# Where a decode kernel's forward loop issues its pair sums, its projection matmuls and its small ScalarE copies

## Chip, cores and metric

The kernel runs on one core of one Trainium2 chip. The metric is the device time of one execution in microseconds; the time before is the median of five runs. A profile of one execution, taken by the hardware profiler, stands beside it.

## What is computed

One token is decoded through an adaptively normalised block, forward and backward. `mod = silu(c) @ w_mod` gives six vectors (shifts, scales, gates). Attention has 32 heads of width 192 over a cache of 8192 keys and values; a second block is a two-layer GELU network with gate. The outputs are the result and the gradients of nine inputs, those of the key and value caches (100 MB each) among them.

```python
h = layernorm(x) * (1 + ca) + sa
q = (h @ wq)                                  # 32 heads of 192
p = softmax(einsum(q, k_cache) * 192 ** -0.5)
x = x + ga * ((p @ v_cache) @ wo)
h = layernorm(x) * (1 + cb) + sb
x = x + gb * B(h)                             # B: x1 = x + ..., x1 + gelu(layernorm(x1) @ w3) @ w4
```

## The kernel before

**Two parts.** A forward part (about 0 to 545 us) streams K and V once, head by head; then come a short dense part (the network and its gradient, to about 590 us) and a backward part, which reads V again and writes both cache gradients. The change lies in the forward part and in the short stretch that ends it.

**Tiling.** A head's 8192 positions lie as 128 partitions by 64. K and V come in two halves of 1536 KB each (`load_k`, `load_v`, on the SP queue). K has a ring of five such buffers, V of three. The weights of a pair of heads (`wo`, 480 KB) and of four heads (`wq`, 960 KB), and chunks of `w_mod` (960 KB), come on the same queue; `wq` and `w_mod` share one buffer.

**Order.** The engines' queues hold exactly the written order (`manual_schedule`). Iteration i of the loop (L504 to L590) works on three heads at once: x = head i (scores), y = head i - 1 (softmax, V scaling, first three quarters of the products with V), z = head i - 2 (last quarter, output). In one iteration:

- VectorE multiplies a half of K by q (`dot_mul`, L297), adds the two halves of the width (`dot_half`, L302); TensorE sums with identity matmuls (`dot_tree`, L308); VectorE reduces the rest (`dot_sum`, L312). This is done for two halves, `pa` and `pb`.
- The maximum goes over the partitions by a matmul into the tile `mx` (L520), and VectorE takes the negative maximum (L526); ScalarE computes the exponentials (L343).
- `scale_v` (L346 to L370) multiplies a quarter of V by the exponentials, nine of 16 steps on VectorE (L356), seven on ScalarE (L363). Tiles `vs`, three buffers.
- `m_quarter` (L387) takes one scaled quarter: TensorE accumulates the 192 by 192 products of K and V in the PSUM tile `mp` (L378, L383) and the head's output in the PSUM tile `op` (L395), the "o bank", of which 193 of 256 columns are used. The tiles `mp` and `op` have two buffers each.
- `m_out` (L419) copies both to SBUF with ScalarE (L414, L416, L422); `m_add` (L425) adds a part on VectorE (L427).

**Once per pair of heads**, at odd i ("last"): `pair_sums` (L436) runs `pair_sum` for both heads, ten fp32 matmuls with one output column (L432 to L434), into a PSUM tile `po` of the one-buffer pool psS. `pair_o` (L442) on VectorE normalises (L444 to L448); `pair_ao` (L451) multiplies with `wo` on TensorE (L455, into `ao_ps`, pool psS), and ScalarE copies the result into `AO` (L557).

**Once per four heads**, at i = 3, 7, ...: `q_half` (L262) runs twice, five matmuls each into `q_ps` (L265; pool psB, one buffer, shared with `mx`), and a scaled ScalarE copy into `qs_bc` (L267), from which the heads i + 1 to i + 4 take their q. At i = 1, 5, 9, `mod_blocks` (L237) does the like for six columns of mod (L241, L242).

**Where these stand.** `pair_sums` and the first `q_half` stand ahead of `m_quarter(1)`. The L557 copy and the second `q_half` or `mod_blocks` stand between `scale_v(2)` and `scale_v(3)`. The loads in an iteration are: K of i + 1, first half (after `m_quarter(3)` of z); V of i, second half (after `scale_v(1)`); K of i + 1, second half (after `m_quarter(1)`); wo, wq or w_mod; V of i + 1, first half. Each waits for the last reader of its buffer, in that order, on SP's one queue.

```python
if last:
    po = pair_sums((os_.pop(i - 3), os_.pop(i - 2)))
if i % 4 == 3 and wch is not None:
    q_half((i + 1) // 4, 0, wch)
if y is not None:
    m_quarter(1, y["k"][0], vs1, y["mp"], y["op"])
nx["k"].append(load_k(i + 1, 1))
```

## Time and profile before

| | |
|---|---|
| median of five runs | 1447.58 us (1443.05 to 1459.39) |
| profiled execution, its own time | 1443.59 us |
| its span, first to last instruction | 1441.8 us |
| mean granted TensorE clock | 0.723 |
| busy in the span: TensorE, VectorE, ScalarE | 83%, 77%, 61% |
| DMA | 571.96 MB, mean 397 GB/s |
| L363, V scaling on ScalarE | 840 of 443 ns, 303.2 us |
| L297, K times q on VectorE | 62 of 3352 ns, 207.8 us |
| L378 and L383, K times V on TensorE | 1920 of 254 ns and 1920 of 251 ns (overlapping), 294.2 us |

The profile counts a matmul as busy to its modelled end, so neighbouring matmuls overlap and the time from start to start is shorter than the mean of one. A line of the timeline gives start, duration, engine, source line, operation, tiles and count, and in brackets the engine's idle time before it and what released it. A line of the waits gives who waited for whom, the total in microseconds, how often, and the longest. Granted clock is TensorE's, as a share of full speed.

### The profile page before, as it was taken

How to read it: one execution, taken by the hardware profiler on the slowest of the kernel's cores; microseconds unless marked ns; L12 is line 12 of the kernel's file. 1: busy time of each engine (PE TensorE's matmuls, PEld its weight loads, DVE VectorE, ACT ScalarE, POOL GpSimd, SP SyncE). 2: the span in 40 equal slices, each digit the busy share in tenths (PEclk: the TensorE clock that was granted, in tenths of full speed). 3: DMA queues.
4: the chain of work that ended last, by engine and by line, in shares of the span. 5: the costliest groups of instructions: out<-in, count | busy, mean ns of one | idle time of the engine just before them, and what ended most of it. 6: DMA issues, size and time to landing. Idle time of an engine off the chain costs nothing.

```text
span 1441.8 us, 29963 instructions
## 1 busy us (share of the span) xinstructions
PE 1194.5 (83%) x12577; PEld 783.8 (54%) x12577; DVE 1109.7 (77%) x1395; ACT 881.2 (61%) x1923; POOL 138.0 (10%) x240
## 2 busy tenths in 40 slices
PE   3999999999999988877888877789887888678874
PEld 1677777677777767544444444445444444344442
DVE  4999999999999997676667676766676677567684
ACT  0777767676777773554555665566566556455654
POOL 0000000000000000121111110111111111011111
PEclk9999999999999997575555555555556556555555
DMA  9999999999999996599999999999999999999998
GB/s 375 398 410 409 415 413 416 390 396 400 391 397 405 410 415 256 200 401 422 418 400 412 422 413 417 418 414 414 408 416 423 425 423 411 370 377 417 400 399 348
DMA packets 77748, 571.96 MB, mean 397 GB/s; under 512 B 8590, under 2 KB 26718, under 8 KB 37294
## 3 DMA queue, kind: packets, MB, share of 16 engines
q1 hardware_dynamic: 51402, 343.59, 59.2%
q0 software_dynamic: 26192, 226.47, 38.0%
q8 instruction: 98, 1.61, 0.4%
q14 instruction: 36, 0.29, 0.0%
q10 hardware_dynamic: 20, 0.00, 0.0%
HBM read 343.58 MB, written 225.91 MB: 395 GB/s over the span
## 4 chain that ended last, share of the span: by engine, by line
PE 44%; DVE 28%; ACT 13%; issue 7%; DMA 7%; POOL 1%; SPq 0%; ACTq 0%; POOLq 0%; DVEq 0%
PE dot_ps L938 18%; DVE prod L297 8%; PE dv_ps L949 6%; DVE pq L929 6%; ACT vs L363 5%; PE wT_ps L816 4%; PE mp L378 4%; DMA out_dram<-KB 3%; DVE prod L302 3%; DVE vs L356 3%; PE dot_ps L308 3%; ACT KB L950 2%; ACT wT L817 2%; PE mp L383 2%; DVE S_h L312 2%
## 5 line engine op out<-in xcount | busy, mean ns | idle before, releaser
L950 ACT CAST KB<-dv_ps 128x768 bf16<-128x768 f32 x504 | 382.4, 803 | 273.7 <-PE dv_ps L949 272.8
L938 PE MATMUL dot_ps<-pq,ident_bf 128*128 128x256 bf16 x1536 | 356.6, 401 | 65.9 <-DVE pq L929 65.6
L363 ACT ACTIVATE vs<-VB,Ef 128x192 bf16<-128x192 bf16 x840 | 303.2, 443 | 0.0
L938 PEld LDWEIGHTS <-ident_bf 128*128 128x128 bf16 x1536 | 188.3, 133 | 189.3 <-issue 128.9
L949 PE MATMUL dv_ps<-do_r,er_b 1*128 1x192 bf16 x2048 | 219.6, 334 | 59.0 <-ACT KB L950 53.2
L954 DVE TENSOR_TENSOR KB<-qs_bc,dS 128x3072 bf16<-128x3072 bf16 x126 | 220.6, 1752 | 24.9 <-DMA out_dram<-KB 19.0
L929 DVE TENSOR_TENSOR pq<-VB,do_r 128x3072 bf16<-128x3072 bf16 x126 | 220.6, 1750 | 0.0
L297 DVE TENSOR_TENSOR prod<-KB,qs_bc 128x6144 bf16<-128x6144 bf16 x62 | 207.8, 3352 | 9.5 <-DMA KB<-in_A_k_cache_dram 4.9
L378 PE MATMUL mp<-vs,KB 128*128 128x193 bf16 x1920 | 190.6, 254 | 0.0
L949 PEld LDWEIGHTS <-er_b 1*128 1x128 bf16 x2048 | 91.9, 111 | 176.8 <-issue 168.9
L378 PEld LDWEIGHTS <-KB 128*128 128x128 bf16 x1920 | 170.9, 101 | 17.4 <-issue 3.9
L312 DVE TENSOR_REDUCE dP<-dot_ps 128x32 f32<-128x512 f32 x64 | 44.2, 690 | 141.5 <-PE dot_ps L938 141.5
L793 POOL DMA_DIRECT2D er_b<-er_t x64 | 40.9, 639 | 1163.4 <-PE w3T_ps L666 576.9
L308 PE MATMUL dot_ps<-prod,ident_bf 128*128 128x512 bf16 x372 | 94.4, 392 | 44.6 <-DVE prod L302 44.6
L356 DVE TENSOR_TENSOR vs<-VB,E 128x1728 bf16<-128x1728 bf16 x120 | 123.6, 1051 | 0.0
L302 DVE TENSOR_TENSOR prod<-prod 128x3072 bf16<-128x3072 bf16 x62 | 108.6, 1752 | 0.6
L817 ACT COPY wT<-wT_ps 128x1024 bf16<-128x1024 bf16 x84 | 80.8, 961 | 45.1 <-PE wT_ps L816 42.1
L383 PE MATMUL mp<-vs,KB 128*64 128x193 bf16 x1920 | 103.6, 251 | 0.0
L383 PEld LDWEIGHTS <-KB 128*64 128x64 bf16 x1920 | 77.6, 110 | 20.1 <-issue 20.1
L308 PEld LDWEIGHTS <-ident_bf 128*128 128x128 bf16 x372 | 34.7, 99 | 86.2 <-issue 58.2
L1187 POOL DMA_DIRECT2D out_dram<-KB x127 | 68.3, 542 | 43.6 <-ACT KB L950 16.1
L343 ACT ACTIVATE E<-S_h,negm 128x256 bf16<-128x256 f32 x30 | 15.2, 508 | 85.7 <-DVE negm L526 85.7
(333 smaller groups left out, 1015.6 us busy)
## 6 DMA issues: line engine op xcount, KB each, us to landing
VB<-in_A_v_cache_dram SPq DMA_DIRECT2D x125, 1536.0 KB, 11.0
out_dram<-KB POOLq DMA_DIRECT2D x125, 1536.0 KB, 14.5
KB<-in_A_k_cache_dram SPq DMA_DIRECT2D x64, 1536.0 KB, 10.3
wo_st<-in_A_wo_dram SPq DMA_DIRECT2D x30, 480.0 KB, 8.6
w_st<-in_A_wq_dram SPq DMA_DIRECT2D x12, 960.0 KB, 13.2
out_dram<-wo_st POOLq DMA_DIRECT2D x16, 480.0 KB, 19.3
out_dram<-w_st POOLq DMA_DIRECT2D x7, 960.0 KB, 21.2
w_st<-in_w_mod_dram SPq DMA_DIRECT2D x6, 960.0 KB, 18.1
```

The lines of the kernel that those rows point to most:

```text
L297: V_.tensor_tensor(out=prod, in0=src, in1=vec[:, None, :].to_broadcast([P, JH, DH]), op=ALU.mult)
L302: V_.tensor_tensor(out=prod[:, :, 0:w], in0=prod[:, :, 0:w], in1=prod[:, :, w : 2 * w], op=ALU.add)
L308: T_.matmul(ps, lhsT=ident_bf, rhs=prod[:, :, k : k + TS], start=(k == 0), stop=(k == w - TS))
L356: V_.tensor_tensor(out=vs[:, 0:n, 0:DH].rearrange("p j (a b) -> p j a b", b=4), in0=v[:, v0 : v0 + n, :].rearrange("p j (a b) -> p j a b", ...
L363: A_.activation(out=vs[:, k, 0:DH], in_=v[:, v0 + k, :], func=ACT.Copy, scale=Ef[:, j0 + k : j0 + k + 1])
L378: T_.matmul(mp[:, 0:MW], lhsT=kb[:, j0 + k, 0:P], rhs=vs[:, k, 0:MW], start=(q == 0 and k == 0), stop=(z and k == JQ - 1), skip_group_chec ...
L383: T_.matmul(mp[p0 : p0 + 64, MO : MO + MW], lhsT=kb[:, j0 + k, P:DH], rhs=vs[:, k, 0:MW], start=False, stop=(z and k >= JQ - 2), skip_grou ...
L929: V_.tensor_tensor(out=pq[:, q], in0=v_l[s][:, q * JQ : (q + 1) * JQ, :], in1=do_of(ht(s)[0])[:, None, :].to_broadcast([P, JQ, DH]), op=AL ...
L938: T_.matmul(ps[:, q * JQ : (q + 1) * JQ, :], lhsT=ident_bf, rhs=pq[:, q, :, k : k + TS], start=(k == 0), stop=(k == DH - TS), skip_group_c ...
L949: T_.matmul(ps[:, b, k * DH : (k + 1) * DH], lhsT=er[p0 : p0 + 1, 2 * m + k, :], rhs=doh[p0 : p0 + 1, :], start=True, stop=True)
L950: A_.copy(out=dV4[:, 2 * q : 2 * q + 2, m * PW : (m + 1) * PW], in_=ps[:, :, 0:PW])
L954: V_.tensor_tensor(out=dK[:, lo:hi, :].rearrange("p j (a b) -> p j a b", b=4), in0=qh.rearrange("p (a b) -> p a b", b=4)[:, None, :, :].to ...
```

## The change

- `pair_sum` runs for one head in every iteration from i = 2 on: at even i for head i - 2, at odd i for the other head of the pair. It stands after `m_quarter(1)` and after the issue of the second K load. It writes columns 200 to 205 of the o bank of the pair's second head, without the start flag; `po` is a view of that bank, and the tile in psS is no longer used.
- At odd i, `pair_o` stands after `dot_half(pb)` and its tree instead of before them.
- The first q half is computed at i = 3, 7, ..., the second at the next (even) i, and mod blocks at i = 2, 6, 10, each with its matmuls between the second dot tree and `m_quarter(2)`.
- The copies into AO, `qs_bc` and `mod` are issued after `scale_v(3)`.
- In the stretch that ends the forward part, the sums of the last two pairs, the second part of head 30's `o_rows`, `pair_o` and `pair_ao` change places.

```diff
-    def mod_blocks(b0, nb, w):
+    def mod_mm(nb, w):
...
+        return ps
+
+    def mod_out(b0, nb, ps):
         A_.copy(out=mod[:, b0 : b0 + nb], in_=ps[:, 0:nb])
...
-    def q_half(n, b, w):
+    def q_mm(b, w):
...
+        return ps
+
+    def q_out(n, b, ps):
         lo = n * CW + b * PW
         A_.activation(out=qs_bc[:, lo : lo + PW], in_=ps[:, 0:PW], func=ACT.Copy, scale=SCALE)
...
-        def pair_sum(po, b, os_h):
+        def pair_sum(po, b, os_h, start=True):
             rows = slice(64 * b, 64 * b + 64)
             for k in range(3):
-                T_.matmul(po[rows, k : k + 1], lhsT=os_h[:, k:DH:3], rhs=c32[:, 0:1], start=True, stop=True)
...
+                T_.matmul(po[rows, k : k + 1], lhsT=os_h[:, k:DH:3], rhs=c32[:, 0:1], start=start, stop=start, skip_group_check=True)
...
-        def pair_sums(os2):
-            po = psS.tile([P, 8], FP32, name="po", tag="s")
-            for b in range(2):
-                pair_sum(po, b, os2[b])
-            return po
...
                 early(i, "mid")
-                if last:
-                    po = pair_sums((os_.pop(i - 3), os_.pop(i - 2)))
-                if i % 4 == 3 and wch is not None:
-                    q_half((i + 1) // 4, 0, wch)
                 if y is not None:
                     m_quarter(1, y["k"][0], vs1, y["mp"], y["op"])
                 nx["k"].append(load_k(i + 1, 1))
+                if z is not None:
+                    po = (z if last else y)["op"][:, 200:208]
+                    pair_sum(po, i % 2, os_.pop(i - 2), start=False)
+                late = []
                 pb = dot_mul(x["k"][1], qh)
                 if z is not None:
                     m_add(i - 2, z["mp"], mt)
+                dot_half(pb)
+                x["d1"] = dot_tree(pb, psR, DH // 2)
                 if last:
                     o2 = pair_o(t, po)
-                dot_half(pb)
-                x["d1"] = dot_tree(pb, psR, DH // 2)
                 if y is not None:
                     vs = scale_v(2, y["v"][1], E4, Ef)
                 if last:
-                    A_.copy(out=AO[:, :, 2 * t : 2 * t + 2], in_=pair_ao(o2, wo_l.pop(t)))
+                    ps_ao = pair_ao(o2, wo_l.pop(t))
+                    late.append(lambda ps=ps_ao, t=t: A_.copy(out=AO[:, :, 2 * t : 2 * t + 2], in_=ps))
                 if i % 4 == 3 and wch is not None:
-                    q_half((i + 1) // 4, 1, wch)
+                    late.append(lambda ps=q_mm(0, wch), n=(i + 1) // 4: q_out(n, 0, ps))
+                if i % 4 == 0 and wch is not None:
+                    late.append(lambda ps=q_mm(1, wch), n=i // 4: q_out(n, 1, ps))
                     wch = None
-                if i % 4 == 1 and wch is not None:
-                    mod_blocks(mb, nb, wch)
+                if i % 4 == 2 and wch is not None:
+                    late.append(lambda ps=mod_mm(nb, wch), lo=mb, n=nb: mod_out(lo, n, ps))
...
                     y["vs"] = scale_v(3, y["v"][1], E4, Ef)
+                for f in late:
+                    f()
                 nx["v"].append(load_v(i + 1, 0, VB[(2 * i + 2) % NVB]))
...
-                if i == H1 - 1:
-                    po = psS.tile([P, 8], FP32, name="po", tag="s")
-                    pair_sum(po, 0, os_.pop(H1 - 3))
...
             score_tree(1, d1)
+            pair_sum(po, 1, os_.pop(H1 - 2), start=False)
             dot_sum(d0, x["S"][:, 0:JH])
             m_add(H1 - 2, z["mp"], mt)
-            o_rows(H1 - 1, vy, op_y, JH, J)
-            o_out(H1 - 1, op_y, es, os_)
...
             mx = row_max(x["S"])
-            po_x = psr([P, 8], FP32, "po_x")
-            pair_sum(po_x, 0, os_.pop(H1 - 1))
+            o_rows(H1 - 1, vy, op_y, JH, J)
+            o2 = pair_o(TL - 1, po)
             negm = neg_max(mx)
             A_.activation(out=E_all[:, H1, :], in_=x["S"], func=ACT.Exp, bias=negm[:, 0:1], scale=1.0)
+            o_out(H1 - 1, op_y, es, os_)
+            ps_ao = pair_ao(o2, wo_l[TL - 1])
+            A_.copy(out=AO[:, :, 2 * TL - 2 : 2 * TL], in_=ps_ao)
+            po_x = psr([P, 8], FP32, "po_x")
             op_x = psO.tile([P, 256], FP32, name="op")
...
-            pair_sum(po, 1, os_.pop(H1 - 2))
-            o2 = pair_o(TL - 1, po)
+            pair_sum(po_x, 0, os_.pop(H1 - 1))
             pair_sum(po_x, 1, os_.pop(H1))
             er_t = [e_rows(TL, psB, "b")]
-            ps_ao = pair_ao(o2, wo_l[TL - 1])
             w3t(1)
             o2 = pair_o(TL, po_x)
-            A_.copy(out=AO[:, :, 2 * TL - 2 : 2 * TL], in_=ps_ao)
```

## The prediction

> **What bounds the kernel now.** I began with the page's slices of the span.

> ```profile
> ## 2 busy tenths in 40 slices
> PE   3999999999999988877888877789887888678874
> ...
> DVE  4999999999999997676667676766676677567684
> ...
> PEclk9999999999999997575555555555556556555555
> DMA  9999999999999996599999999999999999999998
> ```

> The change touches only the forward loop over heads, the first fifteen slices (0 to 545 us). There TensorE, VectorE and DMA all read nine tenths, so busy shares don't tell which of them is the bound. The waits between 65 and 543 us do:

> ```profile
> ACT AO L557 <- PE ao_ps L455: 39.1, 14, 4.6
> PE dot_ps L308 <- DVE prod L302: 29.7, 32, 1.8
> ACT qs_bc L267 <- PE q_ps L265: 21.1, 14, 3.0
> DVE rz L444 <- PE po L434: 13.7, 14, 1.2
> DVE S_h L312 <- PE dot_ps L308: 6.4, 7, 1.6
> ```

> VectorE waits 13.7 us for the pair sums (14 times) and 6.4 us for dot trees (7 times), and almost nowhere else. ScalarE's two large waits cost VectorE nothing directly. So VectorE sets the pace, broken by TensorE once per pair. Next, stretches of one pair each (an odd head and the even one after it; us, length, busy PE, PEld, DVE, ACT, POOL, then granted clock, DMA share, GB/s):

> ```profile
> 304.87:338.96 34.09, 31.74 (x455) 24.79 (x451) 32.27 (x32) 24.22 (x77) 0.00 (x0) 0.95 0.97 383
> 338.96:374.18 35.22, 33.15 (x463) 25.19 (x459) 32.36 (x32) 25.18 (x79) 0.00 (x0) 0.95 1.00 404
> 374.18:407.43 33.25, 29.93 (x451) 23.27 (x449) 32.11 (x31) 24.21 (x77) 0.00 (x0) 1.00 0.99 395
> 475.87:509.44 33.57, 31.51 (x461) 24.18 (x459) 32.34 (x32) 25.18 (x79) 0.00 (x0) 1.00 1.01 417
> ```

> VectorE's work is the same 32.1 to 32.4 us; the lengths differ by the clock. The fourteen pairs from i = 3 last 35.17, 34.63, 33.57, 34.62, 33.57, 34.54, 33.58, 34.09, 35.22, 33.25, 35.18, 33.26, 33.57 and 34.16 us. Clock 0.95 stands at i = 3, 5, 9, 13, 17, 19, 23. In slices of 0.2 us each of these is one stretch of half clock, 3.4 us long, begun during or just after the pair sums (316.2 to 319.8 at i = 17). Last, the timeline of TensorE and VectorE in a pair at full clock (i = 21):

> ```profile
> 382.96 0.52 PE L395 MATMUL op<-vs,ones_bf 128*32 128x193 bf16 x16
> 383.41 0.69 PE L432 MATMUL po<-c,osb 128*64 128x1 f32 x6
> ...
> 385.50 0.38 PE L434 MATMUL po<-osb,c 128*128 128x1 f32 x2
> 385.75 1.51 PE L378 MATMUL mp<-vs,KB 128*128 128x193 bf16 x16
> ...
> 388.42 1.47 PE L308 MATMUL dot_ps<-prod,ident_bf 128*128 128x512 bf16 x6
> ```

> ```profile
> 384.63 0.35 DVE L427 TENSOR_TENSOR M<-mp,mt 64x193 f32<-64x193 f32 x1
> 385.92 0.18 DVE L444 RECIPROCAL rz<-po 128x3 f32<-128x3 f32 x1 [0.94 <-PE po L434]
> ...
> 386.48 1.75 DVE L302 TENSOR_TENSOR prod<-prod 128x3072 bf16<-128x3072 bf16 x1
> 388.14 1.05 DVE L356 TENSOR_TENSOR vs<-VB,E 128x1728 bf16<-128x1728 bf16 x1
> ```

> Both heads' sums stand ahead of the second quarter (L378), and VectorE's in-order queue stands 0.94 us at the reciprocal with its half-add behind it.

> [...]

> **The change, part by part.**

> *Half clock.* [...] So I take the stretches as gone. Their price, against full-clock pairs with q matmuls (33.57) and without (33.25): 1.60 + 1.65 + 1.61 at i = 3, 19, 23; 1.38 + 1.37 + 0.84 at i = 5, 9, 17; 1.29 - 0.5 = 0.8 at i = 13, whose even head has the small operations of L475 to L480. Sum 9.25 us. Ends: 0 if they stay; 9.25.

> *The wait for po.* A walk through i = 21: the second quarter starts at 383.41, lasts 2.67 (385.75 to 388.42), so to 386.08. ScalarE's part of it was done at 383.84, before the tenth of 16 steps needs it. The sum takes 1.11: 387.19, seen by VectorE 0.04 later, 387.23. VectorE has the M add at 384.63, the half-add from 385.01 (0.38 on, as elsewhere), 1.66 more: 386.67. Wait 0.56 in place of 0.94: the wait moves, it doesn't go. 14 x 0.38 = 5.3 us. Ends: 0 (the quarter waits for all of ScalarE's scaling) and 14 x 0.94 = 13.2. Late next is nothing: the dot tree needs the half-add (386.67) and starts at 387.2, 1.2 earlier than now.

> *Even heads.* Their sum stands ahead of their second dot tree, which waits 0.65 us for VectorE at i = 22; the tree comes 0.4 us later, and the reduction that reads it has about a microsecond of room (tree done at 302.9, reduction at 304.0 at i = 16). Zero; without that cover 0.4 x 14 = 5.6.

> *q and mod matmuls.* The same number, one half in each of two heads. Full-clock pairs with q are 0.32 longer; TensorE idles 3.3 us in a pair without, so half of each hides. I take half of 7 x 0.25: 0.9 us. Ends 0 and 2.2.

> *ScalarE copies behind the V scaling.* The waits of 39.1 and 21.1 us shrink, off VectorE's path: nothing by itself. Behind the late q copy wait VectorE's product of head 4n (it reads qs_bc) and the mx matmul, which shares q_ps's bank; scaling ends about 320.5 in a head that ends at 322.5, so the copy at 320.7 to 321.2 has 1.3 us of room. If that is gone, 7 times the excess.

> *Queues.* On SP the second K load follows the second quarter, 2.3 us earlier (3.4 where the clock was halved: issued at 320.35, and 172 to 233 GB/s in the three microseconds after 320). The wo load follows ao, 1.2 earlier, the V load the scaling, 1.5 to 2 earlier. At i = 2, 6, 10 the wq load, and at i = 4, 8 the w_mod load, now wait on SP for a matmul group of their own head, with a V load behind that would wait for the scaling anyway: nothing. POOL issues nothing here.

> *Tail.* Head 30 loses its sum ahead of mx (544.54 to 545.5) and gets one ahead of a tree that waits 0.65; a VectorE wait of 0.58 at 549.64 goes. The later sums and pair_o swap places of equal length. Gain 0.4, ends -0.5 and 0.6.

> VectorE's sum: 9.25 + 5.3 + 0.9 + 0.4 = 15.9 us.

> *What DMA lets through.* The pairs from i = 3 to 9 (with w_mod loads) moved 56.7 MB in 138.0 us. At the densest pair's 417 GB/s that takes 136.0; at 425, which single slices show in the backward part, 133.4. VectorE would save 6.1 there; I allow 3.3, so 2.8 are lost. The later ten moved 137.2 MB in 340.4 us; at 417 that is 329.0, room for 11.4 where VectorE saves about 9.5. Total 15.9 - 2.8 = 13.1 us. Against the profiled execution: 1443.59 (span 1441.8 and 1.8 around it) to 1430.5. That execution is 4.0 below the median of the five; the median's counterpart is 1447.58 - 13.1 = **1434.5**.

> **Rivals.**
> *No DMA limit:* all 15.9 and up to 3 more of the po wait: 1430. For: K transfers never hold VectorE now. Against: 417 is the best of all pairs.
> *The po wait stays or some half clock stays:* half of 9.25 to all of it, nothing else: gain 5 to 9, 1440. [...] Against: the steps start before ScalarE has ended (PE at 311.43 with scaling to 311.96).
> *It doesn't do what it says:* DMA share is 1.00 throughout, so earlier loads only queue and VectorE meets late K: 1446. Against: dry microseconds such as 320 to 323.
> *Slower:* every one of 29 sums starts a half-clock stretch. At 9.25 / 7 = 1.3 us each, 29 x 1.3 = 38 less 15.9: 1470. It needs over 12 stretches to cancel the gain from the other terms, 23 for 1% slower. Against: thin stretches are half as long as now.

> **How the numbers follow.** Forecast 0.46 (own range 1430 to 1438), no DMA limit 0.17, part stays 0.20, nothing 0.08, slower 0.09. Below 1427 and above 1448 I leave about 0.17. One per cent, 14.5 us, is about what a measurement of this kernel can tell from no change. Below 1433.1 lie the no-limit case and half of the forecast: 0.40. Slower by over 1%: 0.08. The rest, 0.52, is within.

> **What would show it.** Right: granted clock 1.00 in all pairs, L444's wait about 0.56 each, no wait at L312, pairs near 32.9 after i = 11, no dry microseconds after the second K load, ScalarE's waits at AO and qs_bc gone. Wrong: half-clock stretches, or VectorE waiting for K transfers in more than the early pairs.

## The result, and the profile after

Each median is over the runs of its own series. The changed kernel takes 1436.65 us (38 runs, 1427.98 to 1448.33), the kernel before, measured beside it, 1446.75 us (75 runs). The ratio on record is 0.9937, with a 95% interval of 0.9923 to 0.995, so 0.6% faster; the quotient of the two medians is a little lower, 0.993. The medians differ by 10.1 us where 13.1 were forecast. The prediction of 1434.5 is 2.2 us low. The profiled execution of the changed kernel took 1433.29 us, with a span of 1431.5; it is 3.4 us below its median, as the one before was 3.2 us below its own.

The slices of the changed kernel's span, to be read against those of before: the first fifteen are the forward loop.

```profile
## 2 busy tenths in 40 slices
...
PEclk7999999999999997755555566565555557555565
...
GB/s 374 405 419 418 419 411 412 413 413 407 418 413 409 418 382 217 238 365 425 421 422 416 419 400 410 423 416 420 409 413 410 421 421 413 419 385 411 402 411 343
```

No forward slice is below 405 GB/s between the second and the fourteenth; before, several were between 390 and 400. A half-clock stretch of 3.4 us in a slice of 36 us is too short for the digit to show it, so the clock has to be read pair by pair. VectorE's waits between 65 and 535 us in the changed kernel (us in all, times, longest):

```profile
DVE rz L444 <- ACT vs L369: 5.1, 10, 0.6
DVE prod L303 <- DMA KB<-in_A_k_cache_dram: 4.9, 9, 1.5
DVE prod L303 <- PE dot_ps L314: 1.7, 1, 1.7
DVE negm L526 <- PE mx L520: 1.2, 1, 1.2
DVE rz L444 <- PE op L440: 0.9, 1, 0.9
```

The wait for the pair sums is 6.0 us instead of 13.7, and the 6.4 us for dot trees are gone. Nine waits for a K transfer are new, and so is the one at L303 for a dot tree; it belongs with the one at L526 (below), where before there were 0.6 us in two places. ScalarE's wait ahead of the AO copy fell from 39.1 us to 1.6, ahead of the q copy from 21.1 to 0.2. ScalarE isn't busier for it: its wait for the negative maximum, ahead of the exponentials, rose from 65.2 to 120.5 us (28 times each), off VectorE's path.

The label "ACT vs L369" in the first row is not the cause. The changed kernel's timeline of the pair i = 21, in order of start:

```profile
376.44 1.52 PE L384 MATMUL mp<-vs,KB 128*128 128x193 bf16 x16
...
377.78 2.53 ACT L369 ACTIVATE vs<-VB,Ef 128x192 bf16<-128x192 bf16 x7
...
378.03 1.76 DVE L308 TENSOR_TENSOR prod<-prod 128x3072 bf16<-128x3072 bf16 x1
...
379.86 0.38 PE L440 MATMUL op<-osb,c 128*128 128x1 f32 x2
...
380.35 0.18 DVE L444 RECIPROCAL rz<-op 128x3 f32<-128x3 f32 x1 [0.56 <-ACT vs L369]
```

ScalarE's scaling ends at 377.78 + 2.53 = 380.31, by coincidence beside the end of the sum; as the loop repeats, so does the coincidence. The test is the distance that does not change: L444 starts 0.49 us after the start of L440 here, and again at 346.87 to 347.36 and 412.85 to 413.34. In experiment e1_sums, where the sum is late and ScalarE was done 0.48 us earlier, it is 0.49 too (348.90 to 349.39), and there the profile names "PE op L440". So VectorE waits for the sum. The reader also sees the new order: quarter (L384), one sum (which ends with L440), and VectorE's half-add (L308) now ahead of the reciprocal instead of behind it.

Pairs of the changed kernel (start and end, length, busy PE, PEld, DVE, ACT, POOL, granted clock, DMA share, GB/s):

```profile
166.41:201.34 34.93, 30.82 (x481) 24.10 (x479) 32.39 (x32) 24.27 (x78) 0.00 (x0) 1.00 1.01 413
334.21:367.20 32.99, 30.54 (x452) 23.46 (x447) 32.21 (x31) 24.70 (x79) 0.00 (x0) 1.00 1.02 419
...
499.15:535.60 36.45, 32.51 (x458) 25.04 (x456) 32.51 (x32) 25.05 (x81) 0.00 (x0) 0.95 0.97 382
```

The thirteen from i = 3 last 34.17, 33.74, 33.42, 34.93, 33.41, 33.50, 32.98, 32.98, 32.99, 32.99, 32.99, 32.98 and 32.99 us, all at clock 1.00. From i = 15 on they are equal to a hundredth, with q matmuls (the row from 334.21) or without (from 367.20, 32.99 us with 461 matmul records, not shown). The first six are longer, though VectorE's and TensorE's work is nearly the same (32.39 and 30.82 us in the first row). Five of them, i = 3 to 11, hold all the K waits; the w_mod loads are issued at heads 0, 4 and 8. The sixth, i = 13, has no K wait but more work of VectorE's own (32.76 us), the small operations that the prediction names. The last row has the only half-clock stretch of the forward loop from head 3 on, and it is longer than its counterpart before.

The two profiled executions by stretch: up to head 3, 65.19 us before and 65.08 after; heads 3 to 29, 444.25 and 434.07 (-10.18); from head 29's first product to du_bf, the end of the work that depends on the forward loop, 70.18 and 73.02 (+2.84); the rest about -2.8. The rest is not touched by the change, and from the write of dao_bf to the end its length varies between 852 and 866 us over the profiles of this study, so -2.8 there is no finding.

What went wrong at the end of the loop shows in the changed kernel's timeline there:

```profile
500.94 0.28 PE L174 MATMUL bc_t<-ident_f,dbo 128*5 128x128 f32 x1
...
502.61 0.21 PE L181 MATMUL bc_ps<-bc_rows,ident_bf 5*128 5x128 bf16 x1 [0.67 <-ACT w4b L182]
...
503.17 0.49 PE L520 MATMUL mx<-ident_f,m 128*128 128x128 f32 x2 [0.35 <-ACT w4b L182]
...
503.50 2.63 PE L384 MATMUL mp<-vs,KB 128*128 128x193 bf16 x16
...
503.70 0.29 DVE L526 TENSOR_REDUCE negm<-mx 128x1 f32<-128x128 f32 x1 [1.20 <-PE mx L520]
...
509.28 3.36 DVE L303 TENSOR_TENSOR prod<-KB,qs_bc 128x6144 bf16<-128x6144 bf16 x1 [1.69 <-PE dot_ps L314]
```

At the end of head 28 the kernel broadcasts the columns of dbo (L174 to L182): TensorE and ScalarE hand over to each other four times, and in that time TensorE does little (0.28 us of the transpose, 0.38 us of a group of four that is not shown, and 0.21, in the 1.9 us from 500.94 to 502.82). Head 28 is a multiple of four, so its second half of q and its sum now stand on TensorE's queue ahead of this. The mx matmuls come late, VectorE waits 1.20 us for them; the quarter behind runs at half clock (2.63 us for what takes 1.5); the dot tree comes late by that, and the next product, which needs the tree's buffer, waits 1.69 us.

### The profile page after: what moved, and what is told of

Same layout as the page of the kernel before. It is cut to its first block, busy times and chain, and to the rows that moved or that the text cites. A ratio compares the mean times of both kernels' runs of the same rounds, so it can differ in the third digit from the quotient of the medians.

```text
span 1431.5 us, 29992 instructions
## 1 busy us (share of the span) xinstructions
PE 1186.7 (83%) x12577; PEld 776.7 (54%) x12577; DVE 1109.7 (78%) x1395; ACT 878.1 (61%) x1923; POOL 137.9 (10%) x240
## 3 DMA queue, kind: packets, MB, share of 16 engines
q8 instruction: 98, 1.61, 0.4%
## 4 chain that ended last, share of the span: by engine, by line
PE 38%; DVE 33%; DMA 11%; ACT 8%; issue 8%; POOL 1%; SPq 0%; ACTq 0%; POOLq 0%; DVEq 0%
PE dot_ps L940 19%; DVE prod L303 10%; PE dv_ps L951 6%; DMA KB<-in_A_k_cache_dram 6%; DVE pq L931 6%; DVE prod L308 4%; PE wT_ps L818 4%; DVE vs L362 4%; DMA out_dram<-KB 2%; ACT vs L369 2%; PE mp L384 2%; ACT wT L819 2%; DVE S_h L318 2%; ACT KB L952 2%; PE dot_ps L314 2%
## 5 line engine op out<-in xcount | busy, mean ns | idle before, releaser
L369 ACT ACTIVATE vs<-VB,Ef 128x192 bf16<-128x192 bf16 x840 | 303.2, 443 | 0.0
L940 PEld LDWEIGHTS <-ident_bf 128*128 128x128 bf16 x1536 | 188.5, 133 | 188.8 <-issue 128.4
L303 DVE TENSOR_TENSOR prod<-KB,qs_bc 128x6144 bf16<-128x6144 bf16 x62 | 207.8, 3352 | 15.3 <-DMA KB<-in_A_k_cache_dram 9.9
L384 PE MATMUL mp<-vs,KB 128*128 128x193 bf16 x1920 | 184.1, 248 | 0.9 <-DVE vs L362 0.9
L384 PEld LDWEIGHTS <-KB 128*128 128x128 bf16 x1920 | 163.8, 98 | 17.3 <-issue 6.5
L362 DVE TENSOR_TENSOR vs<-VB,E 128x1728 bf16<-128x1728 bf16 x120 | 123.6, 1050 | 0.0
L308 DVE TENSOR_TENSOR prod<-prod 128x3072 bf16<-128x3072 bf16 x62 | 108.7, 1753 | 1.0
L314 PEld LDWEIGHTS <-ident_bf 128*128 128x128 bf16 x372 | 37.5, 105 | 86.7 <-issue 58.3
```

What stands on the lines that cost most here:

```text
L303: V_.tensor_tensor(out=prod, in0=src, in1=vec[:, None, :].to_broadcast([P, JH, DH]), op=ALU.mult)
L308: V_.tensor_tensor(out=prod[:, :, 0:w], in0=prod[:, :, 0:w], in1=prod[:, :, w : 2 * w], op=ALU.add)
L314: T_.matmul(ps, lhsT=ident_bf, rhs=prod[:, :, k : k + TS], start=(k == 0), stop=(k == w - TS))
L362: V_.tensor_tensor(out=vs[:, 0:n, 0:DH].rearrange("p j (a b) -> p j a b", b=4), in0=v[:, v0 : v0 + n, :].rearrange("p j (a b) -> p j a b", ...
L369: A_.activation(out=vs[:, k, 0:DH], in_=v[:, v0 + k, :], func=ACT.Copy, scale=Ef[:, j0 + k : j0 + k + 1])
L384: T_.matmul(mp[:, 0:MW], lhsT=kb[:, j0 + k, 0:P], rhs=vs[:, k, 0:MW], start=(q == 0 and k == 0), stop=(z and k == JQ - 1), skip_group_chec ...
```

## The experiments

The theory was the prediction's: the split of the sums removes the half clock and most of the wait; the copies and q matmuls do nothing alone; DMA limits the early pairs; and the broadcasts at head 28 give 2.8 us back. Main rivals: the gain comes from the ScalarE copies; it comes from shorter sums or from their position alone; the early pairs are long for another reason than DMA.

"du_bf" below is the start of that one VectorE operation in the profiled execution, 579.62 us before and 572.17 after: it ends the part that the change can touch.

**One part alone: the sums.** The changed kernel, with the q and mod matmuls and the ScalarE copies back in their old places.

```diff
+if i % 4 == 3 and wch is not None:            # behind early(i, "mid"), as before
+    q_out((i + 1) // 4, 0, q_mm(0, wch))
-    ps_ao = pair_ao(o2, wo_l.pop(t))
-    late.append(lambda ps=ps_ao, t=t: A_.copy(out=AO[:, :, 2 * t : 2 * t + 2], in_=ps))
+    A_.copy(out=AO[:, :, 2 * t : 2 * t + 2], in_=pair_ao(o2, wo_l.pop(t)))
...
+    q_out((i + 1) // 4, 1, q_mm(1, wch))
...
+    mod_out(mb, nb, mod_mm(nb, wch))          # i % 4 == 1, as before
```

> Only the pair sums and pair_o are as after; q, mod and the AO copy stand where they stood before. Theory (the sums' place carries the gain: half clock and po wait): no half-clock stretch at the pair sums, pairs without q matmuls at 32.9 to 33.0 us, pairs with q matmuls at about 33.7 (the first q half again stands ahead of the second quarter, 0.8 us more of po wait), no stall of 2.9 us after head 28; 8 to 10 us below before in all (1437 to 1439 beside 1447). Rival (the moved q matmuls and copies carry it): within 2 us of before, half clock as before.

Measured: 1439.29 us against 1447.49 of the kernel before on the same chip, ratio 0.9951 (0.9932 to 0.9971); du_bf 574.0. From 65 us to the end of the loop the clock is 1.00 throughout. From i = 15 to 26, pairs with q matmuls last 33.8 us, those without 32.98. VectorE's waits between 65 and 535 us:

```profile
DVE rz L444 <- PE op L440: 10.7, 8, 1.7
...
```

(2.9 us more in six places stand under the label of ScalarE.) The sums alone give most of the gain and all of the clock. The rest is seen in that row: where the q matmuls stand in the odd head ahead of the quarter, the sum is late and the wait is 1.37 to 1.7 us (0.76 at i = 15); where they don't, at most 0.56 inside the loop's regular pairs. Moving them to the end of two heads is worth 0.8 us in each late pair that has them, once the sums are split. Behind head 28 there is no stall to speak of here (0.4 us at the negative maximum), which ties that stall to the moved q half.

**The other part alone: q, mod and the copies.** The kernel before, with q_mm, q_out, mod_mm, mod_out and the `late` list as in the change; pair_sums untouched.

> Only q, mod and the small ScalarE copies are as after; both heads' sums stand together ahead of the second quarter, in psS, as before. Theory: the half-clock stretches at the sums stay (five to nine of them in fourteen pairs), the po wait stays at 0.94 to 1.2 us, ScalarE's waits at AO and qs_bc fall from 60 us to under 10, and the stall after head 28 appears (2.5 to 3 us); total within 4 us of before (1443 to 1451 beside 1447). Rival (ScalarE's waits held the V loads and so the pace): 5 to 10 us below before.

Measured: 1448.13 us against 1447.49, ratio 0.9996 (0.9977 to 1.0014); du_bf 580.7. Its waits of VectorE:

```profile
DVE rz L450 <- PE po L440: 13.4, 14, 1.1
DVE prod L303 <- ACT qs_bc L273: 4.6, 6, 0.8
...
DVE prod L303 <- PE dot_ps L314: 1.4, 1, 1.4
DVE negm L532 <- PE mx L526: 1.2, 1, 1.2
```

Without the split of the sums the rest of the change is worth nothing. The wait for po is nearly what it was (13.7). Half clock stands in seven pairs: i = 5, and from i = 7 on strictly every second one (34.9 to 35.0 us; between them 33.26, and 33.75 at i = 13). A new row appears: in the six from i = 7 on, VectorE's product of the next head waits for the late q copy, 4.6 us in all. This is the exposure that the prediction named for these copies ("1.3 us of room. If that is gone, 7 times the excess"), and it opens where a half-clock stretch is in the same pair: the pair i = 3, with q matmuls at full clock, has no such wait. The last two rows are the stall behind head 28, which comes with the moved q half even without the split. ScalarE's waits at AO and q fell to 18.5 and 4.7 us, less than expected, and VectorE gained nothing from it.

**The broadcasts at head 28 moved.** The changed kernel, with the transpose at "mid" of head 28 and the fifth column at "mid" of head 29, so that one group of four matmuls and one copy stay at the end of head 28:

```diff
+    if i == H1 - 3:
+        tp = psS.tile([NF, P], FP32, name="bc_t", tag="s")
+        T_.transpose(out=tp[0:ND, :], in_=dbo, identity=ident_f)
+        bc_rows = tmp.tile([NF, P], BF16, name="bc_rows")
+        A_.copy(out=bc_rows[0:ND, :], in_=tp[0:ND, :])
+    if i == H1 - 2:
+        bc_part(4, 1)
...
-    bcast_cols(dbo, ND, dbo_bc, A_.copy)
+    bc_part(0, 4)
```

> After, with the five broadcasts of dbo at the end of head 28 spread out: transpose and row copy in the middle of head 28, four broadcasts at its end and one in the middle of head 29, all in psS. Theory (these stand behind the q matmuls that head 28 now has, and hold mx by 1.2 us, the second product by 1.7): the wait at L526 in head 29 and the wait of the product for the dot tree go, no half clock there; 2.5 to 3 us below after, the pair from head 29 at about 33.5 us in place of 36.45. Rival (that stretch is set by late K transfers): the pair stays at 35 us or more, VectorE waiting for K.

Measured: 1436.7 us against 1447.49, ratio 0.9929 (0.9899 to 0.9959). The timeline at the same place:

```profile
501.89 0.39 PE L506 MATMUL bc_ps<-bc_rows,ident_bf 5*128 5x128 bf16 x4
...
502.54 1.51 PE L384 MATMUL mp<-vs,KB 128*128 128x193 bf16 x16
...
507.19 3.36 DVE L303 TENSOR_TENSOR prod<-KB,qs_bc 128x6144 bf16<-128x6144 bf16 x1
```

Both waits and the half clock (1.51 instead of 2.63 for the quarter) are gone: from head 29's first product to that of the last head is 34.63 us instead of 37.84, so 3.2 saved. The mechanism is shown. The gain expected in the total is not: only 1.8 of the 3.2 reach du_bf (head 29's product to du_bf 71.21 instead of 73.02), because the loads behind don't come sooner by as much. TensorE waits 1.76 us for a part of w3 instead of 0.59, and VectorE, which needs a product that stands behind it on TensorE's queue (aoN), waits 1.7 us instead of 0.4; the wait for w4a stays (2.2 and 2.3 us), and that for K is 1.0 instead of 0.7. The kernel's time can't be told from that of the changed kernel. In the pair i = 9 a half-clock stretch appears that the changed kernel hasn't (190.6 to 194.1): there TensorE stood idle for 2.04 us for a half-add whose product had waited for K.

**A version with pair_o later as well.** e3_bcast, with pair_o behind scale_v(2), and pair_ao with its wo load behind the third quarter. VectorE then does a V scaling (1.05 us, L362) ahead of the reciprocal, so that the sum is done when VectorE gets there.

```diff
-    if last:
-        o2 = pair_o(t, po)
     if y is not None:
         vs = scale_v(2, y["v"][1], E4, Ef)
+    if last:
+        o2 = pair_o(t, po)
...
```

> As e3_bcast, and pair_o stands behind scale_v(2), pair_ao and the wo load behind the third quarter's matmuls. Theory (0.56 us of po wait per pair is left, and DMA caps at about 417 GB/s): the wait at L444 goes, VectorE alone would take 32.4 us per pair, but at 13.58 MB per pair and 417 GB/s it gets 32.5 to 32.7, with waits for K transfers in all pairs; the early pairs with w_mod loads don't change; 3 to 5 us below e3_bcast. Rival (no DMA cap in the late pairs): 32.4 us per pair and no waits for K after head 15, 6 to 8 us below.

Measured: 1433.29 us against 1447.49, ratio 0.9901 (0.9861 to 0.9941); du_bf 568.1. Its largest wait of VectorE, and one of its pairs:

```profile
DVE prod L303 <- DMA KB<-in_A_k_cache_dram: 6.4, 13, 1.1
```

```profile
431.17:463.58 32.41, 30.27 (x458) 23.52 (x457) 32.18 (x31) 24.23 (x77) 0.00 (x0) 1.00 1.01 416
```

No wait is left at L444; 6.0 us were there in e3_bcast between 65 and 535 us. Heads 3 to 29 take 431.98 us instead of 434.41: 2.4 arrive. K transfers take the largest part of the rest, 6.4 us in thirteen places instead of 4.3 in eight: VectorE now waits for them in late pairs as well, at 416 to 419 GB/s. Two half-clock stretches in place of one, at 121 and 189 us, are there too. This pair of 32.41 us holds 32.18 us of VectorE work: the loop is close to VectorE's limit, and its K waits say that it is close to DMA's too.

**Both sums behind the odd head's quarter.** This keeps the place of the changed kernel's sum and undoes the split over two heads:

```diff
-if z is not None:
-    po = (z if last else y)["op"][:, 200:208]
-    pair_sum(po, i % 2, os_.pop(i - 2), start=False)
+if last:
+    po = z["op"][:, 200:208]
+    pair_sum(po, 0, os_.pop(i - 3), start=False)
+    pair_sum(po, 1, os_.pop(i - 2), start=False)
...
```

> After, but both heads' sums run together at odd heads, behind the second quarter (2.2 us of one-column matmuls in one piece, none at even heads). Theory (the length of the thin stretch triggers half clock, wherever it stands): half-clock stretches of 3.4 us return in four to ten of fourteen pairs, begun at or just behind the sums; po wait 1.6 us where the clock is full, pairs of 34.0 us there and longer where it is halved; 8 to 14 us above after. Rival (it was the place ahead of the quarter, with its wait for the osb copy): clock 1.00 in all pairs, 34.0 us each.

Measured: 1446.3 us against 1446.82 on that chip, ratio 1.0002 (0.9984 to 1.0021); du_bf 581.7. Its largest wait of VectorE, and two of its pairs:

```profile
DVE rz L444 <- PE op L440: 18.7, 12, 1.7
```

```profile
372.62:406.65 34.03, 30.82 (x464) 24.01 (x463) 32.20 (x31) 24.38 (x78) 0.00 (x0) 1.00 0.98 393
440.69:474.82 34.13, 32.16 (x464) 24.46 (x463) 32.19 (x31) 24.37 (x78) 0.00 (x0) 0.95 0.98 376
```

The whole gain is gone. VectorE waits at L444 for 18.7 us in twelve pairs by the label of L440 and for 3.6 in two by ScalarE's, 22.3 over fourteen, 1.6 each: 0.56 and one sum more (1.11) would make 1.67. So the place behind the quarter is no gain by itself; to be behind the quarter pays because only one of the two sums is there. Nor is it the o bank, which this version uses too. Half clock is back as well, in five of fourteen pairs, and yet its price is different: the pair at 440.69, with 3.4 us of half clock, is 0.10 us longer than the one without; the others are longer by 0.05 to 0.54, and the three by 0.53 or 0.54 (i = 3, 7, 27) are those in which VectorE also waits 0.3 to 0.5 us for the late q copy. That TensorE has slack behind VectorE's long wait here, and the stretch uses it up, is my reading and not tested.

**Each sum doubled.** The changed kernel, with the sum written once more into eight other columns of the same bank, so that every head has 2.2 us of one-column matmuls between a quarter and a tree:

```diff
+pair_sum((z if last else y)["op"][:, 208:216], i % 2, os_[i - 2], start=False)
 pair_sum(po, i % 2, os_.pop(i - 2), start=False)
```

> After, with every head's sum run twice, the first into eight unused columns of the o bank (2.2 us thin in every head). Theory: half-clock stretches return, in eight to sixteen of 28 heads, at even heads too; po wait 1.6 us at odd heads with full clock; 18 to 30 us above after, slower than before. Rival (only TensorE's added time counts): clock 1.00, 12 to 18 us above after.

Measured: 1460.94 us against 1446.82, ratio 1.0089 (1.0052 to 1.0126), some 24 us above the changed kernel. Its pairs last 34.4 to 35.9 us; one without a half-clock stretch:

```profile
276.52:310.96 34.44, 32.77 (x471) 25.47 (x469) 32.83 (x36) 24.77 (x79) 0.00 (x0) 1.00 1.01 408
```

Doubling brings the half clock back, eight stretches of about 3.4 us, in even and odd heads, where the changed kernel with its 1.11 us per head has none from i = 3 to 27. So 2.2 us can be followed by half clock; but only eight of 28 groups between 55 and 545 us are. The trace shows which. The half-clock stretches of a profile begin whole multiples of 3.413 us apart: in the kernel before, the seven from 77.36 to 418.70 us begin 0, 10, 30, 50, 70, 80 and 100 such steps after the first, and each is one step long. Lay steps of 3.413 us over the trace of e6_double_sum so that the stretches begin with a step: the eight groups began 0.62 to 1.34 us after the start of a step, and the twenty others up to 0.37 us or from 1.57 us on. So for a group of this length its place in the step tells whether a stretch follows. Most of the loss is not clock: pairs without a stretch are 1.5 us longer as well, from the work itself and the waits for it.

**No w_mod loads.** The changed kernel, with the last wq tile in place of each w_mod tile:

```diff
-wch = load_w(wm_v, mb * P, (mb + nb) * P)
+wch = lw
...
```

> After, without the three w_mod loads in the loop (at heads 0, 4, 8): the mod matmuls read the wq chunk that lies in the buffer, so the values of mod from column 12 on are left out and replaced by others; all instructions on TensorE, VectorE and ScalarE stay. Theory (early pairs are held by 417 GB/s): VectorE's waits for K fall from 4.9 to under 1 us, the pairs from heads 3, 5, 7, 9 fall from 34.17, 33.74, 33.42, 34.93 to 33.0 each, 4 to 5 us below after. Rival (they are longer for another reason, such as the mod matmuls at even heads or the loads' waits on SP): unchanged within 1 us.

Measured: 1433.8 us (four runs) against 1446.82, ratio 0.9884 (0.9853 to 0.9915; the quotient of the medians is 0.991); du_bf 566.7. The pair i = 7, and two of VectorE's waits:

```profile
132.19:165.16 32.97, 31.28 (x459) 24.03 (x457) 32.18 (x31) 24.70 (x79) 0.00 (x0) 1.00 1.01 418
```

```profile
DVE prod L303 <- DMA KB<-in_A_k_cache_dram: 1.8, 5, 0.6
DVE negm L526 <- PE mx L520: 1.2, 1, 1.2
```

VectorE's waits for K fall from 4.9 us to 1.8, not under 1 as expected; the pair i = 3 keeps 1.3 of them and lasts 33.94 us. The pairs i = 5 to 11 fall to 32.97 to 33.00 us, the length of the late ones, though they still do the w_mod matmuls. So DMA is what makes these pairs longer. The pair i = 13 stays at 33.48, as its extra work would have it. Heads 3 to 29 take 430.5 us instead of 434.07, 3.6 us less (2.4 less than in the second profile of the changed kernel, below).

This run also takes the stall behind head 28 apart. The broadcasts delay the maximum by the same 1.2 us, but no half-clock stretch follows (the clock is full until 550 us), and the product doesn't wait. From head 29's first product to that of the last head it takes 36.24 us, against 37.84 in the changed kernel and 35.14 in the kernel before. So of the 2.7 us lost there about 1.1 are the delay itself and 1.6 the stretch behind it.

**The changed kernel and the late pair_o side by side.**

These are the changed kernel as it is, and e4_late_pair_o as it is.

> The kernel after, unchanged, beside the next one on the same chip. Theory: 0.993 of before, pairs of 32.98 us from head 15 on, the pair from head 29 stretched by 3 us, as in its first profile; only the backward part differs from one execution to the next (855 to 866 us from the first gradient column to the end in the profiles so far). Rival (the early pairs' K waits or the clock were chance): half-clock stretches at the pair sums, or early pairs below 33.2 us.

> e4_late_pair_o again, beside after on the same chip. Theory: its forward part ends 4 to 5 us sooner, so its median lies 2 to 6 us below after (ratio to before 0.988 to 0.992). Rival (what the forward part saves is taken back by the late loads of w4 and V): equal to after within 1 us.

Measured: 1435.87 us (ratio 0.991, 0.9884 to 0.9937) and 1432.95 us (0.9883, 0.9848 to 0.9918), against 1449.05 on that chip. The version with the late pair_o is 2.9 us below the changed kernel, the same sign and nearly the size of the 3.4 us between e4_late_pair_o and e3_bcast; the intervals overlap, so it is likely and not shown. Its K waits are 7.9 us in 17 places. It has the lowest median of the study. The changed kernel's second profile has the stall behind head 28 again, 1.2 us at the negative maximum and 1.7 at the product, and its late pairs are again 32.98 to 32.99 us. Its early pairs differ: i = 3 to 9 take 134.75 us instead of 136.26, with 3.7 us of K waits instead of 4.9, and heads 3 to 29 take 432.9 instead of 434.07; du_bf is at 570.25.

## Why the prediction was right, and where it was off

*Half clock, 9.25 us.* Right: no pair from i = 3 to 27 has a stretch, in either of the two profiles of the changed kernel. The 9.25 us rested on my estimate that one sum per head (1.11 us) starts no stretch. No run from before the change shows that; the two profiles of the changed kernel do, where it is put to the test: sixteen single sums began 0.48 to 1.36 us after the start of a step of 3.413 us, inside the range in which every double sum was followed by half clock. How much of the sums lies in one step doesn't explain the stretches alone. For sums that begin late in it this fits (in the kernel before, 1.86 us in the step at i = 27 without a stretch, 1.90 at i = 5 with one); but five groups of e6_double_sum that began in the first 0.37 us of a step lay wholly in it, with 2.2 us, and no stretch came. Why is open.

Ahead of the stretches of the kernel before TensorE was hardly idle: it was without a matmul for 0.24 us in each of the seven steps that precede one (busy 3.17 of 3.41 us). 1.1 us of one-column matmuls per head didn't bring the half clock, and 2.2 us could. A second way to a stretch was not foreseen: where K is late, TensorE idles for the half-add (2.0 us of idle time ahead of the stretch in e3_bcast at 190.6, 2.7 and 2.8 in e4_late_pair_o at 121 and 189).

*The wait for po, 5.3 us.* Right in place: the wait moves to the end of one sum, and 0.55 to 0.56 us are left in six pairs (i = 3 and 19 to 27), as walked through. Elsewhere it is smaller, where something else had held VectorE, and 0.85 behind head 28's stall; in all it fell by 7.7 us, against 5.3 forecast. e5_both_sums_late shows that the split over two heads makes it.

*Even heads, copies and queues, nothing.* Right: no wait at the reductions, and e2_qcopies is worth nothing. *q matmuls, 0.9 us.* The forecast was that half of the 0.32 us between full-clock pairs with and without q would go; all of it went, to 0.01 us. Together with the wait for po the terms fit: pairs without q fell from 33.25 to 32.98 us, those with it from 33.57 to 32.98, which over seven of each is 6.0 us where 6.2 were forecast. The worth of the q move depends on the rest: 0 in e2_qcopies, 0.8 us against e1_sums in each late pair that has them, of which the changed kernel lost a part at head 28.

*The shared o bank.* In the changed kernel L444 reads the sums of 15 pairs (78.2 to 548.3 us) from the o bank with no clearing step, and the values read there are right. That they need none was my assumption: no run from before the change shows it.

*DMA.* The mechanism is right, and shown by e7_no_mod_load. Its size is not settled. From i = 3 to 9 a gain of 3.3 us was allowed; for 138.0 us before, 136.26 were measured in the first profile and 134.75 in the second, so 1.7 and 3.2. The pair i = 11 waits for K too (0.3 us in the first profile, 0.9 in the second), for which nothing was taken off. Together with VectorE's terms the forecast for heads 3 to 29 was 15.9 - 0.4 - 2.8 = 12.7 us, and 10.2 and 11.3 came.

*Tail: this is the step that failed.* "Gain 0.4, ends -0.5 and 0.6." It looked at heads 30 and 31 and at the sums there, and not at the one head in which an edit that was costed at nothing meets other work: head 28 is a head 4n, so the second half of q moves to its end, onto TensorE's queue ahead of the broadcasts. The prediction had named what stands behind the late q copy in such a head, VectorE's product and mx, with 1.3 us of room; the broadcasts use that room up. Cost, head 29's product to du_bf: +2.84 us in the first profile, 2.26 in the second. e1_sums, which doesn't move the q half, needs only 0.2 us more than the kernel before there; e3_bcast removes the local loss of 3.2 us. Part of the size is chance: without the half-clock stretch, as in e7_no_mod_load, it is 0.7.

*The sum.* In the first profile the change is worth 579.62 - 572.17 = 7.45 us up to du_bf, against 13.1 forecast. Missing are 2.5 us in heads 3 to 29 (12.7 forecast, 10.2 found) and 3.2 in the tail (0.4 forecast, -2.84 found). In the second profile it is 9.37. The medians differ by 10.1, so about 2.6 us stand between the first profile and the medians. I can't place them, and they are no constant: the same difference is 2.4 to 2.7 for e1_sums, e3_bcast, e4_late_pair_o and e5_both_sums_late, but 0.1 for e7_no_mod_load, 3.8 for e8_after_again and 4.3 for e9_late_pair_o_again. The part behind du_bf varies by more than that between executions, and there is one profile of the kernel before, whose forward part may have been short for it. This stays open. So the nearness of 1434.5 to 1436.65 is in part luck: 2.6 us come from something that the prediction's sum doesn't contain, and another 0.8 from the median of the kernel before, which was 1447.58 when the prediction was made and 1446.75 in the end.

*The rivals.* "No DMA limit" is excluded by the K waits, "some half clock stays" by the clock, "it doesn't do what it says" by both. "Slower" named the right mechanism: with twice the thin work per head (e6_double_sum) the kernel is indeed slower, though more by the work than by the clock.

## What to carry to other kernels

When a stage repeats, cost an edit in its ordinary turn and then once more in each turn where it meets work that isn't repeated (first, last, and where another stage begins): the largest miss here was one head of thirty. Split a short dependent job over the turns before it is needed, and put only its last part on the path: the same place for the whole job gained nothing. And before adding up VectorE's savings, ask at each size of stage what the transfers need for it: of the 6.0 us of waits that e4_late_pair_o took from VectorE only 2.4 arrived, and K waits took the largest part of the rest.
